# A fused transformer block on one core: a new list for the order of issue of all engines' work

## The chip, the core and the metric

The kernel runs on one core of a Trainium2 chip. Its engines work in parallel, each in the order in which its instructions were issued: TensorE (PE; its weight loads are shown apart as PEld), VectorE (DVE), ScalarE (ACT), GpSimd (POOL) and SyncE (SP), which here issues nearly all transfers. The metric is the device time of one execution in microseconds (us).

## What is computed

The block has 2048 rows of 512 numbers and a conditioning vector `c`. In short:

```
mod = silu(c) @ w_mod                      # six vectors: sa, ca, ga, sb, cb, gb
h   = layernorm(x) * (1 + ca) + sa
q, k, v = h @ wqkv                         # 32 heads of 16
logits[s, w] = q[s] . k[s - 2 w] / 4       # w = 0..7, masked where s - 2 w < 0
o   = softmax(logits) applied to v[s - 2 w]
x   = x + ga * (o @ wo)
h   = layernorm(x) * (1 + cb) + sb
x   = x + gb * ((gelu(h @ w_gate) * (h @ w_up)) @ w_down)      # 1792 hidden
```

Inputs, weights and output are bf16.

## The kernel before, in words

The rows are worked in four groups of 512, numbered 0 to 3 (`sg` in the code). Each group goes through the same chain of small steps. A step is an `Op`: one engine, a function that issues one or a few instructions, and a name (`fire`). The names below are those of the code, and a number behind the first dot is the group:

- `LN1.g.st0` to `st3` (L430, L431, DVE): statistics of a quarter of the rows. Some quarters are done on ACT instead: `sa`, `nm`, `sq` (L408, L414, L419). `vd` and `va` (L460, L465, DVE) add the epsilon, `rs` (L471, POOL) takes the power -1/2, `x0` to `x3` (L448, DVE) normalise.
- The transpose of the normalised rows: by PE for `LN1.1` and `LN2.0` (`t0`, `t1`, L484) and `LN1.0` (`th0` to `th3`, L514), by a transposing transfer from SP for the others (`.t`, L490). `.h0` to `.h3` apply scale and shift: on ACT (L532), on POOL for `LN1.2` (L530), on ACT and DVE for `LN1.0` (L549, L547).
- `qp.g.b.j` (L606, and L579 for the first ones): products for block b (0 = q, 1 = k, 2 = v), part j. `qkv.g.b.j` (L626, L628, L632, ACT) casts each out of PSUM.
- `vst` (L642) writes v to DRAM, `V4.g.0` to `.2` and `V4ld.g` (L651) read it back shifted.
- `pq.g.j` (L671, DVE): products of q and shifted k. `lp.g.j` and `lp.g` (L685, PE) sum them over the head with 32-wide products.
- Softmax: `mx` (L702), `z` (L708), `e` (L713, ACT), `s1` (L718), `ri` (L724), `p` (L729).
- `ptp.0` (L743, PE) spreads the weights for group 0; for groups 1 to 3 `est` (L757) and `ptl`, `pt` (L765) do it through DRAM.
- `pv.g.j` (L778, DVE): weights times v; `o.g.j` (L797, PE) sums them; `oT` (L808, ACT) casts them.
- `x1p` (L818, PE) and `x1` (L827, DVE): output projection and first residual. Then `LN2` as `LN1`.
- `g.g.f` and `u.g.f` (L851, PE), f = 0 to 13; `gl` and `ub` (L885, L892, ACT) take them out of PSUM; `hh` (L903, DVE) multiplies them.
- `y.g.c.0` and `.1` (L863, PE; `yl` L875 at the very end): the down projection in two halves of 7 products; `ot` (L910, `otl` L918, DVE): second residual; `sto` (L935, L926): the store.
- Apart from the groups: `w0` to `w16` (L217), PE warm-up products; `mp0` to `mp5` (L348, L305, L369, PE), the products with `w_mod`, with `mod01` (L355, DVE), `mod3`, `mod4`, `gc2`, `gc5` (ACT) behind them, and `gst`, `ga`, `gb` (SP), which spread the gates; `woS` (L391) and `WdS` (L386, DVE), which multiply the gates into `wo` and `w_down`; the loads `x0` to `x3`, `wm0` to `wm5`, `wqkv`, `wo`, `Wg`, `Wu`, `Wd` (SP).

Buffers are counted in slots that a step takes and gives back: among others four PSUM banks `mm` (for qp, mp, g, u, y), two `att` (o, x1p and transposes), five SBUF buffers for pq and pv, three each for `gl` and `ub`, sixteen for `hh`.

The chains are 135 generators (threads), numbered in the order in which they are spawned. The list `ORDER` (L19) holds 850 thread numbers. `run` takes the list from front to back and issues the next step of the thread named; the engines' queues are thereby written out by hand. A step's dependencies and slots are only asserted there:

```
for i in ORDER:
    op = nxt[i]
    assert all(name in self.done for name in op.after), (op.fire, op.after)
    for s in op.take:
        assert s.n > 0, op.fire
        s.n -= 1
    op.fn()
    for s in op.give:
        s.n += 1
    nxt[i] = next(self.threads[i], None)
```

What an engine waits for while it runs follows from the data and buffers of each instruction.

Of the kernel before, what the change touches and what calls it, by code (L numbers as in the profile page):

```python
# [16 lines left out]
PT_DMA = (1, 2, 3)  # L17

ORDER = [  # L19
# [965 lines left out]
```

## Time and profile before

| what | value |
|---|---|
| median of 3 runs | 238.06 us (238.01 to 238.08) |
| profiled execution: span from first to last instruction | 235.7 us |
| median less that span | 2.36 us |
| PE busy | 229.0 us (97%) |
| DVE busy | 170.0 us (72%) |
| ACT busy | 150.5 us (64%) |
| POOL busy | 23.6 us (10%) |

The page gives no time of the profiled execution beside its span. A group of instructions is named by the line that issued it, its engine, and the tiles that it writes and reads (`out<-in`); `[0.90 <-POOL rstd L471]` behind a row is the idle time of the engine before it, and what ended it. Matmuls overlap in the records, so a PE row's length is longer than the distance to the next one.

### The profile page before, as it was taken

What the parts mean: (1) busy time and instruction counts of PE and PEld (TensorE: products, weight loads), DVE (VectorE), ACT (ScalarE), POOL (GpSimd) and SP (SyncE); (2) the same over time, 40 slices, a digit from 0 to 9 for tenths busy, and PEclk for the clock granted to TensorE, in tenths of its full rate; (3) what the DMA queues carried; (4) which work ended last, traced back from release to release, by engine and by line L of the source; (5) the groups of instructions that cost most, each with busy time, mean ns of one, the idle gap of its engine ahead of it and who ended that gap; (6) DMA issues with size and microseconds to landing.
All of it is one profiled execution on the core that took longest, in us unless ns stands there. A gap on an engine that the chain in (4) does not pass through costs nothing.

```text
span 235.7 us, 3655 instructions
## 1 busy us (share of the span) xinstructions
PE 229.0 (97%) x1376; PEld 108.6 (46%) x1388; DVE 170.0 (72%) x240; ACT 150.5 (64%) x283; POOL 23.6 (10%) x43
## 2 busy tenths in 40 slices
PE   7899899999999999999999999999999999999995
PEld 2755355434644444443444444444444444444443
DVE  3898999999999999989899787259295421222222
ACT  4799978796997558943867592446737325667400
POOL 2525471000100000040000010000001000000000
PEclk9999999999999999999999999999999999999999
DMA  6997987999969929607301972520000061000011
GB/s 212 375 361 210 209 214 138 217 376 347 195 161 241 298 75 201 112 3 178 90 0 32 211 123 48 144 56 0 0 3 1 22 134 45 3 0 0 0 47 45
DMA packets 36265, 30.21 MB, mean 128 GB/s; under 512 B 14872, under 2 KB 34328, under 8 KB 36248
## 3 DMA queue, kind: packets, MB, share of 16 engines
q1 hardware_dynamic: 35968, 29.72, 49.7%
q8 instruction: 11, 0.18, 0.4%
q10 hardware_dynamic: 280, 0.26, 0.3%
q14 instruction: 6, 0.05, 0.1%
HBM read 22.37 MB, written 4.98 MB: 116 GB/s over the span
## 4 chain that ended last, share of the span: by engine, by line
PE 79%; DVE 10%; DMA 5%; POOL 3%; issue 1%; ACT 0%; DVEq 0%; POOLq 0%
PE g_ps L851 21%; PE u_ps L851 21%; PE y_ps L863 14%; PE qkv_ps L606 11%; PE x_ps L818 6%; DMA x<-in_A_x_dram 5%; DVE pq L671 4%; PE o_ps L797 3%; POOL rstd L471 3%; PE LTp L685 2%; DVE xn L448 1%; PE y_ps L875 1%; DVE pv L778 1%; DVE st L430 1%; DVE e L729 1%
## 5 line engine op out<-in xcount | busy, mean ns | idle before, releaser
L851 PE MATMUL g_ps<-h,Wg 128*128 128x512 bf16 x224 | 57.5, 379 | 0.0
L851 PE MATMUL u_ps<-h,Wu 128*128 128x512 bf16 x224 | 57.5, 379 | 0.0
L863 PE MATMUL y_ps<-Wd,hht 128*128 128x512 bf16 x203 | 45.6, 379 | 0.4
L885 ACT ACTIVATE gl<-g_ps 128x512 bf16<-128x512 f32 x56 | 33.7, 601 | 17.5 <-PE g_ps L851 15.4
L892 ACT CAST ub<-u_ps 128x512 bf16<-128x512 f32 x56 | 32.9, 587 | 16.2 <-PE u_ps L851 16.1
L606 PE MATMUL qkv_ps<-hT,wqkv 128*128 128x512 bf16 x180 | 41.0, 380 | 0.0
L903 DVE TENSOR_TENSOR hht<-gl,ub 128x512 bf16<-128x512 bf16 x56 | 23.0, 421 | 24.4 <-ACT ub L892 24.4
L778 DVE TENSOR_TENSOR pv<-PT,V 128x4096 bf16<-128x4096 bf16 x16 | 36.0, 2288 | 3.0 <-DMA PT<-escr 3.0
L671 DVE TENSOR_TENSOR pq<-qT,kT 128x4096 bf16<-128x4096 bf16 x16 | 36.4, 2296 | 0.0
L851 PEld LDWEIGHTS <-Wg 128*128 128x128 bf16 x224 | 21.7, 98 | 26.9 <-issue 1.3
L851 PEld LDWEIGHTS <-Wu 128*128 128x128 bf16 x224 | 21.7, 98 | 26.8 <-issue 0.8
L863 PEld LDWEIGHTS <-hht 128*128 128x128 bf16 x210 | 20.6, 98 | 24.7
L606 PEld LDWEIGHTS <-wqkv 128*128 128x128 bf16 x180 | 19.6, 114 | 18.6 <-issue 2.3
L471 POOL TENSOR_TENSOR rstd<-rstd,neghalf 128x4 f32<-128x4 f32 (+1 forms) x9 | 12.8, 1427 | 149.0 <-DVE rstd L460 77.6
L910 DVE TENSOR_TENSOR ot<-y_ps,x 128x512 bf16<-128x512 f32 x15 | 10.2, 690 | 20.0 <-PE y_ps L863 19.8
L532 ACT ACTIVATE h<-h,modT,scl 128x512 bf16<-128x512 bf16 x12 | 8.8, 805 | 20.3 <-DMA h<-xn 20.3
L818 PE MATMUL x_ps<-woP,oT 128*128 128x512 bf16 x60 | 15.1, 379 | 0.2
L430 DVE BATCH_NORM_STATS2 st<-x 128x6 f32<-128x512 bf16 x19 | 12.9, 677 | 3.1 <-DMA x<-in_A_x_dram 2.9
L827 DVE TENSOR_TENSOR x<-x_ps,x 128x512 bf16<-128x512 f32 x16 | 10.8, 688 | 5.4 <-PE x_ps L818 5.3
L808 ACT CAST oT<-o_ps 128x512 bf16<-128x512 f32 x16 | 8.8, 588 | 4.3 <-PE o_ps L797 4.3
L408 ACT ACTIVATE gl<-x 128x512 bf16<-128x512 bf16 x13 | 8.3, 645 | 3.2 <-DVE x L827 2.9
L685 PE MATMUL LTp<-pq,Mph 128*32 128x512 bf16 x128 | 9.1, 382 | 1.3 <-DVE pq L671 1.3
(85 smaller groups left out, 184.7 us busy)
## 6 DMA issues: line engine op xcount, KB each, us to landing
V<-vscr SPq DMA_DIRECT2D x12, 520.0 KB, 10.5
wm<-in_w_mod_dram SPq DMA_DIRECT2D x6, 512.0 KB, 5.3
vscr<-vT SPq DMA_DIRECT2D x4, 512.0 KB, 4.3
out_dram<-ot SPq DMA_DIRECT2D x15, 128.0 KB, 1.7
Wg<-in_B_w_gate_dram SPq DMA_DIRECT2D x1, 1792.0 KB, 9.8
Wu<-in_B_w_up_dram SPq DMA_DIRECT2D x1, 1792.0 KB
wqkv<-in_A_wqkv_dram SPq DMA_DIRECT2D x3, 512.0 KB, 8.8
x<-in_A_x_dram SPq DMA_DIRECT2D x3, 512.0 KB, 9.2
```

What stands on the lines that cost most here:

```text
L430: nc.vector.bn_stats(out=st[:], in_=src()[:, c4, :])
L471: nc.gpsimd.tensor_tensor(out=k["rstd"][:, a:b], in0=k["rstd"][:, a:b], in1=neghalf[:, a:b], op=ALU.pow)
L606: nc.tensor.matmul(ps[:], lhsT=wqkv[blk][:, dt, j::4], rhs=B["hT", sg][:, :, dt, :], start=(dt == 0), stop=(dt == DT - 1))
L671: nc.vector.tensor_tensor(out=pq[:], in0=_ap(B["qT", sg][:, j, :], [[0, W], [1, SG]]), in1=_ap(kT[:, j, sg % 3 * SG + 2:sg % 3 * SG + 2 + ...
L685: nc.tensor.matmul(B["LT", sg][H * g:H * g + H, 4 * t:4 * t + 4, :], lhsT=M[:], rhs=B["pq", sg, j][:, 4 * t:4 * t + 4, g * P:(g + 1) * P], ...
L778: nc.vector.tensor_tensor(out=t[:], in0=_ap(B["PT", sg][:, 0, :], [[SG, 2], [0, 4], [1, SG]]), in1=_ap(v[:, 0, j, :], [[8, 2], [4 * (SG + ...
L818: nc.tensor.matmul(ps[:], lhsT=B["oT", sg][:, j, c4::CPS] if sg else B["oT", sg][:, j, c4 * P:(c4 + 1) * P], rhs=woP[:, j, :], start=(j == ...
L851: nc.tensor.matmul(ps[:], lhsT=Wt[:, dt, ft * P:(ft + 1) * P], rhs=B["h2T", sg][:, :, dt, :], start=(dt == 0), stop=(dt == DT - 1))
L863: nc.tensor.matmul(ps[:], lhsT=B["hh", sg, ft][:, c4 * P:(c4 + 1) * P], rhs=B["Wd", ft // 4][:, ft % 4, :], start=(ft == 0), stop=(ft == F ...
L885: nc.scalar.activation(out=gl[:], in_=B["g", sg, ft][:], func=ACT.Gelu_apprx_tanh)
L892: nc.scalar.copy(out=ub[:], in_=B["u", sg, ft][:])
L903: nc.vector.tensor_tensor(out=hh[:], in0=B["gl", sg, ft][:], in1=B["ub", sg, ft][:], op=ALU.mult)
```

## The change

Only the list `ORDER` differs. It holds the same 850 entries in another order, found by a search that used each operation's duration as a trace shows it. No step, tile, transfer or wait in the code is added, removed or altered. The diff replaces 41 lines of numbers; its beginning:

```
@@ -17,41 +17,41 @@
 ORDER = [
-    23, 23, 23, 23, 23, 23, 23, 2, 33, 1, 23, 1, 0, 23, 0, 22, 31, 23, 23, 31, 31, 2, 33, 22, 23, 23, 22, 23,
-    33, 33, 33, 33, 2, 33, 23, 23, 22, 22, 22, 33, 34, 34, 34, 34, 35, 35, 22, 36, 3, 30, 23, 6, 35, 35, 4, 0,
...
+    23, 0, 0, 2, 33, 33, 23, 23, 23, 23, 23, 23, 23, 23, 23, 23, 1, 1, 22, 22, 23, 23, 23, 23, 31, 22, 31, 33,
+    33, 33, 34, 34, 33, 31, 33, 33, 34, 34, 0, 35, 23, 23, 35, 2, 2, 22, 22, 22, 22, 30, 35, 23, 35, 30, 30, 30,
...
```

Written out by step names, each engine's queue changes as follows (parts that stay as they were are left out; `..` stands for steps in between).

PE:

```
before: w13 w14 mp1 mp0 th0 th1 w15 th2 th3 w16 | qph.0 ..
after:  w13 th0 w14 w15 th1 mp1 mp0 th2 w16 th3 | qph.0 ..
before: qp.0.2.0 qp.0.2.1 qp.0.2.2 LN1.1.t0 qp.0.2.3 t1 mp2 mp3 qp.0.1.3 lp.0.0 qp.1.0.0 qp.1.1.0
        qp.1.2.0 qp.1.2.1 qp.1.2.2 lp.0.1 lp.0.2 lp.0 qp.1.2.3 qp.1.0.1 ..
after:  qp.0.2.0 LN1.1.t0 qp.0.2.1 qp.0.2.2 qp.0.2.3 t1 lp.0.0 mp2 qp.0.1.3 mp3 qp.1.0.0 qp.1.1.0
        lp.0.1 qp.1.2.0 qp.1.2.1 qp.1.2.2 qp.1.2.3 lp.0.2 lp.0 qp.1.0.1 ..
before: qp.1.1.3 qp.2.0.0 .. qp.2.2.2 ptp.0 qp.2.2.3 .. qp.2.1.2 lp.1.0 qp.2.0.3 qp.2.1.3 lp.1.1 o.0.0
        lp.1.2 o.0.1 qp.3.0.0 qp.3.1.0 o.0.2 o.0.3 .. qp.3.0.1 mp4 qp.3.1.1 ..
after:  qp.2.0.0 .. qp.2.2.1 qp.1.1.3 qp.2.2.2 ptp.0 lp.1.0 lp.1.1 qp.2.2.3 .. qp.2.0.3 mp5 o.0.0
        lp.1.2 o.0.1 mp4 qp.2.1.3 qp.3.0.0 qp.3.1.0 o.0.2 o.0.3 .. qp.3.0.1 qp.3.1.1 ..
before: u.0.8 o.1.1 o.1.2 lp.2.2 lp.2 o.1.3 g.0.9 x1p.1.0 x1p.1.1 u.0.9 x1p.1.2 x1p.1.3 g.0.10 ..
after:  u.0.8 g.0.9 o.1.1 o.1.2 lp.2.2 lp.2 o.1.3 u.0.9 x1p.1.0 x1p.1.1 g.0.10 x1p.1.2 x1p.1.3 ..
before: lp.3.0 lp.3.1 lp.3.2 g.1.0 .. u.1.6 g.1.7 o.2.0 o.2.1 lp.3 o.2.2 o.2.3 u.1.7 g.1.8 x1p.2.0 ..
after:  lp.3.0 lp.3.1 g.1.0 .. u.1.4 lp.3.2 o.2.0 o.2.1 g.1.5 .. u.1.6 o.2.2 lp.3 o.2.3 g.1.7 x1p.2.0 ..
before: y.1.2.1 y.1.3.0 y.1.3.1 g.2.0 .. u.2.5 o.3.0 .. o.3.3 g.2.6 .. x1p.3.0 .. x1p.3.3 g.2.8 ..
after:  y.1.2.1 g.2.0 o.3.0 .. o.3.3 u.2.0 g.2.1 x1p.3.0 .. x1p.3.3 .. u.2.3 y.1.3.0 y.1.3.1 g.2.4 ..
before: g.2.11 .. u.2.13 y.2.0.0 .. y.2.3.1 g.3.0 ..
after:  g.3.0 to g.3.3 and u.3.0 to u.3.3 spread between u.2.10 and y.2.2.0
```

DVE:

```
before: st2 LN1.0.vd2 va2 x0 x1 x2 x3 mod01 ..            after: st2 x0 x1 vd2 va2 x2 x3 mod01 ..
before: LN1.2.st1 st2 vd0 LN1.1.x0 x1 x2 LN1.2.va0 LN1.1.x3 pq.0.0 ..
after:  LN1.2.st1 LN1.1.x0 x1 x2 x3 LN1.2.st2 vd0 va0 pq.0.0 ..
(then the same, apart from one or two neighbours, up to pq.2.2)
before: pv.1.1 pv.1.2 pv.1.3 hh.0.5 mx.2 hh.0.6 hh.0.7 WdS0 x1.1.0 x1.1.1 WdS1 hh.0.8 ..
after:  pv.1.1 hh.0.5 pv.1.2 pv.1.3 WdS0 WdS1 WdS2 hh.0.6 hh.0.7 hh.0.8 x1.1.0 x1.1.1 mx.2 ..
before: z.2 LN2.1.va0 pq.3.1 LN2.1.x0 .. x3 ot.0.0 ot.0.1 s1.2 ri.2 p.2 pq.3.2 ot.0.2 ot.0.3 pq.3.3
        hh.1.0 hh.1.1 pv.2.0 hh.1.2 pv.2.1 pv.2.2 hh.1.3 hh.1.4 pv.2.3 hh.1.5 ..
after:  z.2 LN2.1.va0 LN2.1.x0 .. x3 s1.2 ri.2 p.2 ot.0.0 ot.0.1 pq.3.1 pq.3.2 ot.0.2 pq.3.3
        pv.2.0 hh.1.0 hh.1.1 hh.1.2 pv.2.1 hh.1.3 hh.1.4 pv.2.2 pv.2.3 hh.1.5 .. x1.2.0 ot.0.3 ..
after, from there: s1.3, ri.3, p.3 ahead of hh.1.7; pv.3.0 to pv.3.3 ahead of ot.1.0; ot.1.3 ahead of hh.2.2
```

ACT: `scT` ahead of `LN1.0.nm`; `LN1.2.sa3` ahead of the casts `qkv.0.0.j` (before: behind them); `LN1.1.h0`, `h1` ahead of `qkv.0.2.1`; `LN1.3.sq` ahead of `qkv.1.0.1`; `qkv.2.0.2`, `qkv.2.1.2` and `gc5` between `LN1.3.h1` and `h2`; `LN2.1.sa0`, `sa1` ahead of `gl.0.9`; `e.3` behind `gl.1.7` (before: behind `gl.1.9`); `oT.3.j` ahead of `gl.2.0`; `LN2.3.h0` to `h3` between `ub.2.6` and `gl.2.9`. There are seven changes of function between silu, exp and gelu in both lists.

SP:

```
before: .. x1 wqkv1 x2 wqkv2 wm2 wm3 x3 wo2 wo0 wo3 wo1 vst.0 LN1.2.t V4.0.0 gst2 V4.0.1 ga vst.1
        V4.0.2 V4ld.0 LN1.3.t vst.2 wm4 Wg Wu V4.1.0 V4.1.1 V4.1.2 est.1 V4ld.1 ptl.1 Wd0 wm5 Wd1 vst.3 ..
after:  .. x1 x2 wqkv1 wqkv2 wm2 wm3 wo3 x3 Wg vst.0 LN1.2.t V4.0.0 V4.0.1 vst.1 gst2 wo2
        V4.0.2 ga V4ld.0 wm5 LN1.3.t wm4 wo0 vst.2 wo1 Wu V4.1.0 V4.1.1 V4.1.2 vst.3 V4ld.1 gst5 est.1 Wd0 ptl.1 ..
```

Later on SP: `est.2` ahead of `sto.0.0`; `est.3` ahead of `V4ld.3`, and `ptl.3` ahead of `LN2.2.t`; the stores `sto.0.3` and `sto.1.3` go back. POOL's queue is the same in both.

66 rows, old and new, of the table ORDER are left out of this document.

## The prediction

> **What bounds the kernel now.** I read the page first, then the busy time by stretch, the chain of work that ended last, the waits, and the order of time around each wait of TensorE. From the page, and from the busy time by stretch (columns: stretch, length, then busy us and count of PE, PEld, DVE, ACT and POOL, granted clock, DMA share, GB/s):
>
> ```profile
> span 235.7 us, 3655 instructions
> PE 229.0 (97%) x1376; PEld 108.6 (46%) x1388; DVE 170.0 (72%) x240; ACT 150.5 (64%) x283; POOL 23.6 (10%) x43
> ```
>
> ```profile
> 20.00:98.00 78.00, 76.94 (x553) 36.46 (x552) 76.65 (x79) 63.72 (x133) 9.75 (x7) 1.00 0.89 218
> 112.00:233.00 121.00, 120.47 (x623) 55.42 (x629) 65.28 (x106) 64.59 (x105) 2.05 (x2) 1.00 0.21 48
> ```
>
> PE is busy nearly throughout, at a granted clock of 1.00. Until 98 us DVE is equally full (76.65 of 78 us), so there two engines pace the kernel together; after 112 us only PE does. A new order can't shorten PE's work. It can only take out PE's waits, and there are few. From the order of time and the chain:
>
> ```profile
> 27.03 1.05 PE L685 MATMUL LTp<-pq,Mph 128*32 128x512 bf16 x16
> 28.82 0.61 PE L685 MATMUL LTp<-pq,Mph 128*32 128x512 bf16 x8 [0.74 <-DVE pq L671]
> ```
>
> ```profile
> 50.92 0.61 PE L797 MATMUL o_ps<-pv,Msum 128*32 128x512 bf16 x8
> 51.75 0.62 PE L797 MATMUL o_ps<-pv,Msum 128*32 128x512 bf16 x8 [0.21 <-DVE pv L778]
> ```
>
> ```profile
> 110.50 1.05 PE L685 MATMUL LTp<-pq,Mph 128*32 128x512 bf16 x16
> 112.08 0.62 PE L685 MATMUL LTp<-pq,Mph 128*32 128x512 bf16 x8 [0.53 <-DVE pq L671]
> 112.63 1.04 PE L851 MATMUL g_ps<-h,Wg 128*128 128x512 bf16 x4
> ```
>
> ```profile
> 165.32 1.84 PE o_ps L797 x32
> 167.17 0.97 PE g_ps L851 x4
> 168.13 0.86 PE u_ps L851 x4
> ```
>
> A full step (four 128x512 products) takes 0.86 us from start to start. A narrow step (eight 32-wide products: lp, o) takes 0.43, and a group of narrow steps costs about 0.2 more in entering (1.84 for four is 0.11 over 4 x 0.43) and leaving (0.97 against 0.86). So lp.0 lost 28.82 - 27.03 - 0.86 = 0.92 us waiting for pq.0.3, o.0.3 lost 51.75 - 50.92 - 0.43 = 0.40 for pv.0.3, and lp.3.2 lost 112.08 - 110.50 - 0.86 = 0.72 for pq.3.2. Together 2.0 us: about all that an order can win behind the head.
>
> **The change, stage by stage.** I keep count by PE's lateness: the start of a step less the PE work queued ahead of it.
>
> *Head (0 to 13 us).* DVE now makes LN1.0.x0 and x1 ahead of the two small steps vd2 and va2; the transposes th0, th1 stand ahead of mp1, mp0; and the load of x2 is issued ahead of wqkv1.
>
> ```profile
> 7.01 0.73 DVE L448 TENSOR_SCALAR xn<-x,mv,rstd 128x512 bf16<-128x512 bf16 x2
> 7.17 0.80 POOL L471 TENSOR_TENSOR rstd<-rstd,neghalf 128x2 f32<-128x2 f32 x1 [0.34 <-DVE rstd L465]
> 8.01 0.41 DVE L448 TENSOR_SCALAR xn<-x,mv,rstd 128x512 bf16<-128x512 bf16 x1 [0.27 <-POOL rstd L471]
> 8.66 0.17 DVE L355 TENSOR_TENSOR mod<-modT_ps,c 128x8 f32<-128x8 f32 x1
> 9.02 1.77 DVE L547 TENSOR_SCALAR hT<-hTp,mod 128x256 bf16<-128x256 bf16 x5 [0.19 <-PE hTp L514]
> 9.81 2.78 PE L579 MATMUL qkv_ps<-hT,wqkv 128*128 128x256 bf16 x24
> 10.84 0.69 DVE L430 BATCH_NORM_STATS2 st<-x 128x6 f32<-128x512 bf16 x1
> 12.55 2.03 ACT L626 CAST qT<-qkv_ps 128x512 bf16<-128x512 f32 x4
> 14.65 0.66 ACT L408 ACTIVATE gl<-x 128x512 bf16<-128x512 bf16 x1
> ```
>
> POOL's power (0.80) can start only after x0 and x1, so 0.65 later; x0 itself moves up by 0.1. x2 then starts at about 8.67 instead of 8.01, mod01 at 9.34, the five hT writes at 9.55, and LN1.1.st0 at 11.19 instead of 10.84: DVE is 0.35 late. PE's first product starts at 10.0 instead of 9.81. On ACT LN1.2.sa3 (0.66) moves ahead of the four casts, so the casts start at 13.44 instead of 12.55, the first bank comes free at 14.0, and PE, which has four, waits 0.57 for it. The later landing of wqkv1 lies under that wait. Cost: DVE 0.35; PE 0.19 + 0.57.
>
> *13 to 98 us.* lp.0.0 and lp.0.1 come earlier, and qp.1.2.3 moves ahead of lp.0.2 and lp.0, whose wait (0.92) is then filled: by qp.1.0.1 PE is 0.26 ahead. But DVE's work here is the same, in almost the same order, and full, so what is tied to it comes no sooner:
>
> ```profile
> 38.17 1.23 DVE L729 TENSOR_TENSOR e<-LTp,rinv 128x1024 bf16<-128x1024 f32 x1
> 39.85 0.62 PE L743 MATMUL PTp<-e,ident 128*32 128x256 bf16 x16
> 62.22 0.73 DVE L448 TENSOR_SCALAR xn<-x,mv,rstd 128x512 bf16<-128x512 bf16 x2
> 63.00 1.06 PE L484 MATMUL hTp<-ident,xn 128*128 128x128 bf16 x16
> ```
>
> p.0 ends at 39.40 + 0.35 = 39.75, so ptp.0 starts at 39.8, as before (39.85). Mod products mp4, mp5 and the late qp.2.1.3 fill the wait at o.0.3 (0.40), but LN2.0.x3 ends at 62.95 + 0.35 = 63.3, so the transposes LN2.0 end 0.3 later in time with 0.22 more done (mp5). Through 98 us (hh early or late, g.0.9 ahead of o.1.1, WdS ahead) PE keeps a backlog of steps whose inputs exist. DVE's 0.35 goes into the 1.35 us that it idles in this stretch. I take the net at y.0.0.0 as -0.1 (ends: -0.4, if the transposes don't wait; +0.5, if ACT's moved casts each cost one 0.5 us bank wait).
>
> *DMA, the same stage.* Wg (1792 KB) moves from behind LN1.3.t to ahead of vst.0; three wo loads move behind it, wm5 ahead of LN1.3.t. All are on SP's queue, and whatever stands behind them is pushed back.
>
> ```profile
> 10.00:20.00 10.00, 10.00 (x68) 6.68 (x67) 9.52 (x24) 9.64 (x25) 3.94 (x4) 1.00 1.07 344
> 20.00:22.00 2.00, 2.00 (x44) 1.22 (x40) 1.22 (x4) 2.00 (x4) 0.74 (x1) 1.00 0.19 60
> 40.00:42.00 2.00, 2.00 (x24) 1.07 (x17) 2.00 (x4) 2.00 (x4) 0.00 (x0) 1.00 0.02 4
> 49.00:54.00 5.00, 4.74 (x35) 1.93 (x33) 5.00 (x4) 4.26 (x10) 0.00 (x0) 1.00 1.02 412
> ```
>
> ```profile
> 40.75 1.68 SPq L490 DMA_TRANSPOSE hT<-xn  x1
> 45.14 2.94 ACT L532 ACTIVATE hT<-hT,mod 128x512 bf16<-128x512 bf16 x4 [1.22 <-DMA hT<-xn]
> ```
>
> The queue runs empty at 20 and at 40 us. At 412 GB/s Wg takes 4.45 us; less 1.1 for the wo loads (384 KB at the 344 GB/s of 10 to 20 us) it ends 3.4 after 20.0, and 2 of that were empty: vst.0 and all V loads come 1.4 later. That, wm5 (1.4) and wo2 (0.35) must fit into the 2 empty us before LN1.3.t: 1.1 over. The queue's mean share from 20 to 98 us is 0.89, so the 18 us between hold some 2 us in which it could do more; I take 0.9 of them. So LN1.3.t lands 0.2 later, plus DVE's 0.35 on its input, and ACT's h0 starts at 45.65. Ends: 0 and +4.2 (if Wg moves at the mean rate, 218 GB/s). PE's qp.3.0.0 waits for it and starts at 49.75 (before: 49.08, with 0.6 less done); a later landing is paid one to one. The Trainium skill, page "DMA: Bandwidth & Descriptors", section "Where 436 GB/s comes from", says that loads from HBM are bound at about 358 GB/s for a core. By it Wg would take 5.1 us, 0.65 more, and the time would be some 0.4 worse than my sum; the 412 above stands against it.
>
> *98 to 128 us, where the gain is.* LN2.1.x0 to x3 and softmax 2 now stand ahead of pq.3.1; lp.3.2 goes behind u.1.4 with o.2.0 and o.2.1; ot.0.3 goes far back.
>
> ```profile
> 37.30 1.01 POOL L471 TENSOR_TENSOR rstd<-rstd,neghalf 128x4 f32<-128x4 f32 x1 [3.43 <-DVE rstd L465]
> 100.92 2.92 POOL L471 TENSOR_TENSOR rstd<-rstd,neghalf 128x4 f32<-128x4 f32 x1 [39.39 <-DVE rstd L465]
> 103.88 1.38 DVE L448 TENSOR_SCALAR xn<-x,sums,rstd 128x512 bf16<-128x512 bf16 x4 [0.90 <-POOL rstd L471]
> 109.74 2.94 ACT L532 ACTIVATE h<-h,modT,scl 128x512 bf16<-128x512 bf16 x4 [6.89 <-DMA h<-xn]
> 109.75 2.28 DVE L671 TENSOR_TENSOR pq<-qT,kT 128x4096 bf16<-128x4096 bf16 x1
> 116.92 0.42 DVE L903 TENSOR_TENSOR hht<-gl,ub 128x512 bf16<-128x512 bf16 x1 [1.15 <-ACT ub L892]
> 124.87 2.29 DVE L778 TENSOR_TENSOR pv<-PT,V 128x4096 bf16<-128x4096 bf16 x1
> ```
>
> Without pq beside it the power takes 1.01, not 2.92: x0 starts at 102.1 instead of 103.88, and h is ready 1.9 sooner, at 110.8. DVE's idle stays about 1 us. From x0 DVE needs 109.75 - 103.88 = 5.87 us for the same steps before its next pq, so pq.3.1 runs from 107.97 to 110.25, in time for lp.3.1 (110.8), and g.1.0 starts at 111.35. Before, it started at 112.63 with 0.43 more done: 0.85 won. Lost again: one more narrow group, 0.2. pv.2.3 ends at 125.85 (before 127.16; less the 1.15 of idle and ot.0.3's 0.6, plus some 0.4 of waits for the power and for ub.1.4) and o.2.3 is reached at 125.9. Net -0.65; ends -0.85 (no extra group cost) and 0 (o.2.3 waits 0.65 for DVE). ot.0.3's bank is held till 130 us, and three banks are enough while a cast (0.6) is shorter than a step (0.86).
>
> *128 us to the end.* e.3, p.3, pv.3.x and o.3.x come some 15 us earlier, x1p.3.x likewise; y.1.3 and ot.1.3 move, and g.3.0 to g.3.3 go between y.2.x. Cost nothing: PE has 120.47 of 121 us before and the same steps after, DVE only 65.28. Its cover is PE's backlog; were pv.3.3 later than about 153.5, each us would cost one. Number of table loads (7), and the tail from y.3.0.0 on, are unchanged.
>
> Sum: -0.1 (to 98 us), -0.65, and some 0.15 added for arrivals that I found in time by under 0.1: -0.6. The page gives only the span of the profiled execution; the median, 238.06, is 2.36 above it, and I keep that: 235.1 + 2.36 = 237.5.
>
> **Rivals.**
> *Nothing to measure.* o.2.3 meets pv.2.3 with 0.05 to spare, and DVE's lateness of 0.35 must vanish before 98 us. If it doesn't, o.2.3 waits that much, and 0.2 elsewhere: 238.0. For it: both paces are the same engines as before. Against: the idle that takes it up is in the trace.
> *Slower, by the DMA queue.* The transpose LN1.3.t lands over 2 us late behind Wg and wm5; ACT stands before h0 with casts behind it and PE's four banks full, so PE loses 1.7 at qp.3.0.0, of which 0.3 is taken up by 63 us: -0.6 + 1.4 = +0.8, 238.9. It decides from a lateness of about 1.1. For it: LN1.3.t was ACT's wait already (1.22). Against: the empty 2 us.
> *Slower, by POOL.* LN1.2.h3 on POOL and pq.1.1 on DVE overlap. If POOL stands still under pq, as the power did (2.92 against 1.01), qp.2.0.0 waits 2 us: 239.0. The Trainium skill, page "GPSIMD Engine Reference", section "1. Specifications", has POOL share its SBUF interfaces with such DVE instructions. In this trace all POOL work before it is tied to the same pq, and the overlap stays.
> *More.* DVE isn't late and no transition is added: -1.2, 236.9.
>
> **How the numbers follow.** Forecast 0.40; nothing to measure 0.27; DMA 0.20; POOL 0.06; more 0.07. A measurement tells 0.2%, 0.48 us, from no change. The forecast lies just past it and counts a fifth to "same", a little of "nothing" counts to faster: faster 0.42, same 0.32, slower 0.26. The range reaches from the best case to the DMA rival, 236.9 to 239.0.
>
> **What would show it.** Right: lp.0 without its wait; LN1.1.st0 at about 11.2; the power before LN2.1.x0 near 1 us; g.1.0 at about 111.3; no wait at lp.3.2; PE full from 112 us on. Wrong: ACT before LN1.3.h0 much past 46 us, a PE gap before qp.2.0.0 or qp.3.0.0, o.2.3 or any o.3.x waiting for DVE, DVE waiting for V or PT.

## The result, and the profile after

The changed kernel is slower. It takes 240.94 us in the median (239.72 to 241.11), against 238.03 for the kernel before: a ratio of 1.0115, with a 95% interval of 1.0092 to 1.0138. The forecast was 237.5 with a range of 236.9 to 239.0: the time went the other way and lies above the range. A second measurement (below, `after_again`) gave 1.0093 (1.0060 to 1.0126). In the tables below the medians are of all executions and the ratios leave out disturbed ones, so the two can differ a little.

From the page of the changed kernel:

```profile
span 238.8 us, 3651 instructions
...
PE 231.0 (97%) x1377; PEld 109.0 (46%) x1388; DVE 170.2 (71%) x240; ACT 148.7 (62%) x283; POOL 18.6 (8%) x43
```

The profiled execution took 241.05 us, 2.25 over its span, as before (2.36); so the whole difference is in the span, 238.8 against 235.7. I follow it by PE's lateness, the start of a step less the PE work queued ahead of it, as the prediction did. The table is of one execution of each kernel:

| step | before | after | after less before |
|---|---|---|---|
| first product `qph.0` | 4.17 | 4.07 | -0.1 |
| `qp.1.0.1` (after's start 29.82) | 5.79 | 5.34 | -0.45 |
| `o.0.0` (46.72) | 6.34 | 6.03 | -0.3 |
| `qp.3.2.0` (56.70) | 7.08 | 10.85 | +3.8 |
| `g.0.0` (70.40) | 7.46 | 11.14 | +3.7 |
| `y.0.0.0` (102.02) | 8.00 | 11.70 | +3.7 |
| `y.1.0.0` (145.85) | 9.23 | 12.36 | +3.1 |
| last product | 9.47 | 12.60 | +3.1 |

So the new order is ahead until 46 us, loses 4.1 us in the ten that follow, and wins 0.6 back between 98 and 146. The stage of the loss, in busy time by stretch (columns: stretch, length, then busy us and count of PE, PEld, DVE, ACT and POOL, granted clock, DMA share, GB/s), first before, then after:

```profile
44.00:57.00 13.00, 12.73 (x103) 5.01 (x102) 13.00 (x9) 9.46 (x19) 0.00 (x0) 1.00 1.00 361
```

```profile
20.00:22.00 2.00, 2.00 (x37) 1.24 (x35) 1.33 (x5) 1.98 (x4) 0.63 (x1) 1.00 1.03 406
...
44.00:57.00 13.00, 10.19 (x97) 4.23 (x96) 12.30 (x6) 6.96 (x14) 0.00 (x0) 0.87 1.07 305
...
48.00:50.00 2.00, 0.61 (x8) 0.12 (x7) 2.00 (x2) 2.00 (x6) 0.00 (x0) 1.00 1.05 342
50.00:52.00 2.00, 0.97 (x18) 0.70 (x19) 2.00 (x2) 2.00 (x4) 0.00 (x0) 0.81 1.03 322
52.00:54.00 2.00, 2.00 (x7) 0.61 (x5) 1.67 (x2) 0.84 (x2) 0.00 (x0) 0.50 0.98 347
54.00:56.00 2.00, 2.00 (x15) 0.79 (x17) 2.00 (x2) 0.59 (x1) 0.00 (x0) 0.83 1.02 403
```

The queue, empty at 20 to 22 us before, is now full there with Wg (406 GB/s). At 44 to 57 us PE is busy for 10.19 us of 13 instead of 12.73. From 48 to 51 it hardly works, and from about 51 to 55 it works at half its clock: the granted clock falls to 0.50. The order of time in the changed kernel shows what it waits for (start, length; in brackets the idle time ahead and what ended it):

```profile
22.67 4.38 SPq L490 DMA_TRANSPOSE hT<-xn  x1
...
40.71 4.54 SPq L490 DMA_TRANSPOSE hT<-xn  x1
...
44.37 8.90 DVE L778 TENSOR_TENSOR pv<-PT,V 128x4096 bf16<-128x4096 bf16 x4 [1.53 <-DMA V<-vscr]
...
47.34 1.52 ACT L532 ACTIVATE hT<-hT,mod 128x512 bf16<-128x512 bf16 x2 [3.09 <-DMA hT<-xn]
...
48.92 0.61 PE L797 MATMUL o_ps<-pv,Msum 128*32 128x512 bf16 x8 [1.16 <-DVE pv L778]
...
51.03 0.57 PE L305 MATMUL modT_ps<-scT,wm 128*128 128x1 bf16 x16 [1.49 <-DMA wm<-in_w_mod_dram]
...
51.46 4.33 PE L606 MATMUL qkv_ps<-hT,wqkv 128*128 128x512 bf16 x12
```

In the kernel before, the first of the two transposes and `pv.0.0` stand so:

```profile
22.23 1.68 SPq L490 DMA_TRANSPOSE hT<-xn  x1
...
42.80 4.50 DVE L778 TENSOR_TENSOR pv<-PT,V 128x4096 bf16<-128x4096 bf16 x2
```

Three transfers are late at once. V is late for `pv.0.0` (44.37 against 42.80), and behind it PE waits 1.16 us at `o.0.1`. The transpose LN1.3.t is late for ACT's `h0` (47.34 against 45.14). The weights wm4 are late for `mp4`, which the change put ahead of `qp.2.1.3`, so that PE stands 1.49 us more. Then come three steps of four products, x12, that take 4.33 us instead of 2.76 (the same group in `a_fill` below). And SP stands for 4.4 and 4.5 us at the issue of the two transposes, where it stood for 1.68.

This standing makes LN1.3.t late, for its issue starts when it did before (40.71 against 40.75). Where the transfer that was issued ahead of it on SP's queue is still in flight, the issue ends close to that transfer's landing (times in us; in the kernel before it had landed already, and the issue took 1.68):

| run | LN1.3.t: issue starts, ends | issued ahead of it, lands | `h0` starts |
|---|---|---|---|
| before | 40.75, 42.43 | V4ld.0, 40.99 | 45.14 |
| after | 40.71, 45.25 | wm5, 45.46 | 47.34 |
| `a_wg_late` (below) | 40.83, 43.79 | wm5, 43.96 | 45.77 |
| `a_wm5_late` (below) | 40.88, 43.92 | V4ld.0, 44.09 | 45.75 |

In `a_ga_behind` and `a_wg_est` end and landing are 0.6 and 0.4 apart. LN1.2.t behind vst.0 shows the same: after, its issue ends at 27.05 and vst.0 lands at 27.39; before, 23.91 and 24.14. It isn't the whole rule: a later transpose in the changed kernel holds SP from 107.07 to 110.27, though the transfer ahead of it had landed at 103.43.

The other stage in which the two differ is 98 to 146 us. Before, and then after:

```profile
98.32 12.25 PE L863 MATMUL y_ps<-Wd,hht 128*128 128x512 bf16 x54
...
142.72 3.62 PE L863 MATMUL y_ps<-Wd,hht 128*128 128x512 bf16 x15
```

```profile
102.02 12.25 PE L863 MATMUL y_ps<-Wd,hht 128*128 128x512 bf16 x54
...
104.62 1.01 POOL L471 TENSOR_TENSOR rstd<-rstd,neghalf 128x4 f32<-128x4 f32 x1 [38.86 <-DVE rstd L465]
...
123.92 0.62 PE L685 MATMUL LTp<-pq,Mph 128*32 128x512 bf16 x8
...
145.85 0.38 PE L863 MATMUL y_ps<-Wd,hht 128*128 128x512 bf16 x1
```

From `y.0.0.0` to `y.1.0.0`, the same steps, it takes 145.85 - 102.02 = 43.83 us instead of 44.40: 0.57 won. The power takes 1.01 us, not 2.92, and `lp.3.2` (123.92) no longer waits.

### The profile page after: what moved, and what is told of

It is laid out like the page before. It is cut to its first block, busy times and chain, and to the rows that moved or that the text cites. A ratio compares the mean times of both kernels' runs of the same rounds, so it can differ in the third digit from the quotient of the medians.

```text
span 238.8 us, 3651 instructions
## 1 busy us (share of the span) xinstructions
PE 231.0 (97%) x1377; PEld 109.0 (46%) x1388; DVE 170.2 (71%) x240; ACT 148.7 (62%) x283; POOL 18.6 (8%) x43
## 4 chain that ended last, share of the span: by engine, by line
PE 89%; DMA 6%; ACT 2%; SPq 1%; issue 1%; DVE 0%
PE g_ps L851 20%; PE u_ps L851 20%; PE y_ps L863 19%; PE qkv_ps L606 16%; PE x_ps L818 6%; DMA x<-in_A_x_dram 3%; PE LTp L685 3%; PE o_ps L797 3%; DMA wm<-in_w_mod_dram 2%; PE y_ps L875 1%; PE hTp L484 1%; ACT gl L408 1%; ACT oT L808 0%; SPq L245 0%; PE modT_ps L305 0%
## 5 line engine op out<-in xcount | busy, mean ns | idle before, releaser
L863 PE MATMUL y_ps<-Wd,hht 128*128 128x512 bf16 x204 | 46.1, 379 | 0.3
L903 DVE TENSOR_TENSOR hht<-gl,ub 128x512 bf16<-128x512 bf16 x56 | 22.3, 420 | 29.8 <-ACT ub L892 29.6
L606 PE MATMUL qkv_ps<-hT,wqkv 128*128 128x512 bf16 x180 | 42.5, 390 | 0.4 <-ACT qT L626 0.4
L471 POOL TENSOR_TENSOR rstd<-rstd,neghalf 128x4 f32<-128x4 f32 (+1 forms) x9 | 10.5, 1168 | 139.7 <-DVE rstd L465 75.7
L626 ACT CAST qT<-qkv_ps 128x512 bf16<-128x512 f32 x16 | 9.2, 596 | 3.1 <-PE qkv_ps L606 3.1
```

Source lines behind the costliest of these rows:

```text
L606: nc.tensor.matmul(ps[:], lhsT=wqkv[blk][:, dt, j::4], rhs=B["hT", sg][:, :, dt, :], start=(dt == 0), stop=(dt == DT - 1))
L863: nc.tensor.matmul(ps[:], lhsT=B["hh", sg, ft][:, c4 * P:(c4 + 1) * P], rhs=B["Wd", ft // 4][:, ft % 4, :], start=(ft == 0), stop=(ft == F ...
L903: nc.vector.tensor_tensor(out=hh[:], in0=B["gl", sg, ft][:], in1=B["ub", sg, ft][:], op=ALU.mult)
```

## The experiments

My theory after the result: the load Wg (1792 KB), put ahead of vst.0, takes 4.4 us of the DMA engines in a stage that had none to spare, so that V, LN1.3.t and wm4 all come late, and PE's gap then halves its clock. The rivals: it is `ga`, at which SP stands for 5.2 us ahead of V4ld.0; it is `wm5`, put ahead of LN1.3.t; it is `mp4`, put ahead of `qp.2.1.3`; or the new order of PE, DVE and ACT costs the time itself. All kernels below compute the whole block. In some of them the list is a line longer or code is added, so that their line numbers are up to 4 higher.

| label | what it is | median us | ratio to before | 95% interval |
|---|---|---|---|---|
| `a_wg_late` | after, Wg late | 240.68 | 1.0113 | 1.0083 to 1.0143 |
| `b_wg_early` | before, Wg early | 242.30 | 1.0183 | 1.0170 to 1.0196 |
| `a_ga_behind` | after, ga behind V4ld.0 | 240.04 | 1.0060 | 1.0035 to 1.0085 |
| `a_mp4_late` | after, mp4 late | 239.58 | 1.0076 | 1.0060 to 1.0093 |
| `a_wm5_late` | after, wm5 and mp5 late | 238.90 | 1.0034 | 1.0021 to 1.0046 |
| `a_fill` | after, six products in PE's gap | 239.93 | 1.0080 | 1.0066 to 1.0094 |
| `a_sp_back` | after, SP's queue as before | 237.81 | 0.9989 | 0.9979 to 0.9999 |
| `b_98` | before to 98 us, then after | 237.60 | 0.9984 | 0.9974 to 0.9994 |
| `b_wg_half` | before, half of Wg early | 239.93 | 1.0077 | 1.0051 to 1.0102 |
| `a_wg_est` | after, Wg late, est.1 ahead | 238.02 | 0.9994 | 0.9978 to 1.0010 |
| `a_sp_back2` | as a_sp_back, two steps more | 237.46 | 0.9978 | 0.9963 to 0.9993 |
| `b_98_lp` | as b_98, qp.1.2.3 moved | 237.49 | 0.9974 | 0.9960 to 0.9987 |
| `b_wg_act` | before, Wg early on ACT's queue | 242.32 | 1.0180 | 1.0152 to 1.0208 |
| `b_wg_behind_t` | before, Wg behind LN1.2.t | 243.18 | 1.0210 | 1.0181 to 1.0239 |
| `a_wg_act` | after, Wg on ACT's queue | 241.37 | 1.0144 | 1.0103 to 1.0185 |
| `after_again` | after, measured again | 241.15 | 1.0093 | 1.0060 to 1.0126 |

**Wg alone, put early.**

```
 SP (before):  .. wo1
+              Wg
               vst.0 LN1.2.t V4.0.0 .. LN1.3.t vst.2 wm4
-              Wg
               Wu ..
```

> The kernel before with one step moved: Wg is issued ahead of vst.0, all else as it was. Queue theory: vst.0 lands at 27 to 28 instead of 24.1, V4ld.0 and LN1.3.t 1.5 to 3 us later than 41.0 and 45.05, and the time is 239 to 241. Rivals (ga, or wm5 and mp4, which are where they were before): 237.8 to 238.3, since the empty stretches at 20 and 40 us take Wg up.

It costs 4.4 us (1.0183), more than the whole change. The transposing transfer's issue now takes 7.21 us, and everything behind it on SP is late:

```profile
21.95 7.21 SPq L491 DMA_TRANSPOSE hT<-xn  x1
...
47.15 8.90 DVE L779 TENSOR_TENSOR pv<-PT,V 128x4096 bf16<-128x4096 bf16 x4 [2.95 <-issue]
48.63 2.93 ACT L533 ACTIVATE hT<-hT,mod 128x512 bf16<-128x512 bf16 x4 [2.78 <-DMA hT<-xn]
```

`pv.0.0` starts 4.35 later than before and `h0` 3.5. So this one step is enough for a loss of this size, with `ga`, `wm5` and `mp4` where they stood before.

**Wg alone, put back.**

```
 SP (after):  .. x3
-             Wg
              vst.0 .. LN1.3.t wm4 wo0 vst.2 wo1
+             Wg
              Wu V4.1.0 V4.1.1 V4.1.2 vst.3 V4ld.1 gst5 est.1 Wd0 ptl.1.0 ..
```

> The changed kernel with one step moved: Wg (1792 KB) is issued behind wo1, just ahead of Wu, where the kernel before had it, and no longer ahead of vst.0. Queue theory (Wg in front pushes vst.0, the V loads, LN1.3.t and wm4 back, and PE pays at 46 to 57 us): vst.0 lands at about 24, V4ld.0 at 41 to 42 instead of 44.3, LN1.3.t at 45 to 45.5 instead of 47.25; PE's lateness at g.0.0 falls from 11.14 to about 7.1 and the time to 236.9 to 237.6, below both kernels. Rival by ga (SP stands 5.2 us before ga with V4ld.0 behind it): V4ld.0 still lands past 43.5, 239.5 to 240.9. Rival by mp4 (PE waits for wm4 ahead of qp.2.1.3): wm4 is still late behind wm5 and wo2, 239.5 to 240.5.

The loss at 46 to 57 us is gone: `h0` starts at 45.77, `pv.0.0` at 42.88, and PE's lateness at `LN2.0.t0` is 7.41 (before 7.46, after 11.10).

```profile
42.88 8.90 DVE L778 TENSOR_TENSOR pv<-PT,V 128x4096 bf16<-128x4096 bf16 x4
...
45.77 1.52 ACT L532 ACTIVATE hT<-hT,mod 128x512 bf16<-128x512 bf16 x2 [1.41 <-DMA hT<-xn]
```

But the time is hardly better than the changed kernel's. It lies in the range of the rival by `ga`, whose sign did not come (V4ld.0 landed at 42.76, not past 43.5): 2.7 us are lost at another place that I hadn't foreseen.

```profile
67.20 0.35 SPq L757 DMA_DIRECT2D escr<-e  x1
...
74.89 2.57 SPq L765 DMA_DIRECT2D PT<-escr  x4
...
79.58 2.29 DVE L778 TENSOR_TENSOR pv<-PT,V 128x4096 bf16<-128x4096 bf16 x1 [2.60 <-DMA gB<-gscr]
```

(The row names gB as the last to arrive, but `pv.1.0` doesn't read gB; it needs PT.) The write `est.1` is issued at 67.20, and its reads only at 74.89, when it has landed. Ahead of it in the new SP order stand Wg, Wu, vst.3, V4ld.1 and gst5. In the changed kernel est.1's reads followed it after 2.3 us (70.59 and 72.91). So the two ends of the new transfer order belong together: the early Wg had made room for vst.3 and others ahead of est.1.

**Wg back, and what stood ahead of est.1 put behind its reads.**

```
 SP (a_wg_late):  .. V4.1.2
-                 vst.3 V4ld.1 gst5
                  est.1
+                 V4ld.1
-                 Wd0
                  ptl.1.0 ptl.1.1 ptl.1.2 pt.1.1
+                 Wd0 vst.3 gst5
                  gb ..
```

> The changed kernel with Wg issued behind wo1 (as in the kernel with Wg alone put back, 240.7), and behind that the transfers that stand ahead of est.1 or of its reads moved behind them: V4ld.1 behind est.1, and Wd0, vst.3 and gst5 behind pt.1.1. Queue theory: est.1 lands 2 to 3 us after its issue instead of 7.3, ptl.1.0 is issued by 71, pv.1.0 waits under 0.3: 237.6 to 238.4, and the runs scatter less. Rival (pv.1.0's wait came of something else, gB or the earlier lateness): 239.5 to 240.9.

The ratio is 0.9994 and `pv.1.0` no longer waits; ptl.1.0 is issued at 71.42. The reading of the second loss holds, although est.1 still takes longer than I expected (3.8 us from issue to the reads).

```profile
67.66 0.36 SPq L757 DMA_DIRECT2D escr<-e  x1
...
71.42 2.53 SPq L765 DMA_DIRECT2D PT<-escr  x4
...
77.36 2.28 DVE L778 TENSOR_TENSOR pv<-PT,V 128x4096 bf16<-128x4096 bf16 x1
```

**ga, wm5 and mp4, one at a time.**

```
 a_ga_behind, SP:  .. V4.0.2
-                  ga
                   V4ld.0
+                  ga
                   wm5 LN1.3.t ..
 a_mp4_late, PE:   .. o.0.1
-                  mp4
                   qp.2.1.3 .. qp.3.0.1
+                  mp4
                   qp.3.1.1 ..           (ACT: mod4 behind qkv.3.0.1)
 a_wm5_late, SP:   .. V4ld.0
-                  wm5
                   LN1.3.t wm4 wo0 vst.2 wo1
+                  wm5
                   Wu ..                 (PE: mp5 behind qp.3.0.3, ACT: gc5 behind qkv.3.0.3)
```

> The changed kernel with one step moved: ga, which makes SP wait for gst2's landing (32.31 to 37.53), is issued behind V4ld.0 instead of ahead of it. Queue theory: V4ld.0 is issued 5 us sooner, but the bytes ahead of it and of LN1.3.t are the same, LN1.3.t lands at 46.5 or later: 240.0 to 240.9. Rival by ga: V4ld.0 lands by 41, pv.0.0 starts at about 42.8 again, and with it PE's loss at o.0.0 and o.0.1 goes: 238 to 239.

> The changed kernel with mp4 (the product that waits 1.49 us for wm4) put back behind qp.3.0.1, and mod4 with it. Queue theory: PE does qp.2.1.3 at 49.5, then waits for LN1.3.h0 all the same (h0 at 47.3, its four steps and the casts behind it); 0.3 to 1.0 won, 240.0 to 240.6. Rival by mp4: with mp4 gone PE has no gap over 1.5 us, the clock stays at 1.00, and qp.3.0.0 starts at about 50.5: 238 to 239.

> The changed kernel with wm5 (512 KB) issued behind wo1 instead of ahead of LN1.3.t, and mp5 with its cast behind qp.3.0.3; Wg stays in front. Queue theory, in which bytes count: LN1.3.t and wm4 land 1.0 to 1.4 sooner (h0 at about 46), V4ld.0 as late as it was (44.3): 239.0 to 240.5. Rival (wm5 is the main thing): h0 at 45.2 and no loss past 1 us at 46 to 57 us, 237.5 to 238.5.

Only `wm5` wins clearly. With `ga` behind (1.0060) `pv.0.0` starts at 43.48 instead of 44.37 and `h0` stays at 47.32; but its executions scatter from 238.07 to 243.46, and its interval, like that of `a_mp4_late`, overlaps with the second measurement of the changed kernel. With `wm5` behind (1.0034) it is the other way round:

```profile
44.17 8.90 DVE L778 TENSOR_TENSOR pv<-PT,V 128x4096 bf16<-128x4096 bf16 x4 [1.15 <-ACT qT L626]
45.75 1.52 ACT L532 ACTIVATE hT<-hT,mod 128x512 bf16<-128x512 bf16 x2 [1.36 <-DMA hT<-xn]
```

`h0` is 1.6 earlier and the kernel wins about 2 us of the 2.7, a little more than the 0.4 to 1.9 that I expected of 512 KB. With `mp4` late (1.0076) the next wait shows: PE reaches `x1p.0.0` and stands there for the gate multiply, which waits for a wo load that was also moved behind:

```profile
55.16 1.22 DVE L391 TENSOR_TENSOR woP<-woP,gB 128x2048 bf16<-128x2048 bf16 x1 [1.80 <-DMA woP<-in_A_wo_dram]
56.45 1.90 PE L818 MATMUL x_ps<-woP,oT 128*128 128x512 bf16 x8 [1.43 <-DVE woP L391]
```

So none of the three is the whole cause, and each theory was half right. I read them as three places at which one backlog is paid; their parts don't add up to the loss, and no run separates them fully.

**The clock.** Six products that nobody reads go into PE's queue ahead of `mp4`'s, to fill the gap:

```
@@ in cols(b)
-            ps = T("mm", [P, 4], F32, "modT_ps")
+            ps = T("mm", [P, D], F32, "modT_ps")
             B["mp", b] = ps
+            for _ in range(6 * (b == 4)):
+                nc.tensor.matmul(ps[:], lhsT=wqkv[0][:, 0, 0:P], rhs=wqkv[0][:, 0, :], start=True, stop=True)
```

> The changed kernel with six products of 128x512 that nobody reads put into PE's queue ahead of mp4's products (they need no wm4), so that PE works through most of the 1.49 us in which it stands for wm4. Clock theory (the half clock at 51 to 55 us is the price of PE's gaps and is 1.3 to 1.6 of the loss): granted clock 1.00 at 52 to 54 us, qp.2.1.3 to qp.3.1.0 in 0.86 each, 239.3 to 239.7. Rival (the clock costs nothing that the next wait, for h and woS, would not have cost): 240.6 to 241.1.

```profile
50.00:52.00 2.00, 1.84 (x21) 0.80 (x19) 2.00 (x2) 2.00 (x5) 0.00 (x0) 1.00 1.07 319
52.00:54.00 2.00, 2.00 (x20) 1.15 (x17) 1.93 (x1) 1.50 (x4) 0.00 (x0) 1.00 1.02 302
```

```profile
50.13 1.47 PE L304 MATMUL modT_ps<-wqkv 128*128 128x512 bf16 x5
...
52.12 2.76 PE L608 MATMUL qkv_ps<-hT,wqkv 128*128 128x512 bf16 x12
```

The clock stays at 1.00 and the three steps take 2.76 us. The median is 1.0 us below the changed kernel's first one, less than expected, and the interval overlaps with that of its second measurement. The changed kernel's own executions are the better evidence. Measured twice, six of them show a mean clock of 1.000 and take 239.28 us in the mean (238.43 to 240.38); seven show 0.993 and take 241.21 (240.82 to 241.75); three show 0.986 and take 243.03 to 243.55. A mean of 0.993 is 3.3 us at half clock (2 x 0.007 x 238), about the stretch in the profile (51 to 55 us), and it costs PE some 1.7; 0.986 is twice that. So the clock after the gap makes most of the scatter and, where it comes, 1.9 us of the loss; at full clock the changed kernel is still some 1.3 us slower than the kernel before. The mean alone doesn't say where the half clock lies: in the profiled execution of `b_98`, also at 0.993, it is at 9 to 12 us. And the filled kernel, at full clock, is 0.6 slower than the changed kernel's executions at full clock; why is open. The Trainium skill, page "TensorE: Matmul & The Clock Gate", Part 1, says that TensorE falls to half its clock after an idle window of about 3.4 us, and that the window runs freely, so that it varies from run to run. The length and the scatter agree: by the rows of the changed kernel above the half clock lasts (0.19 + 0.50 + 0.17) x 2 / 0.5 = 3.4 us. An idle window isn't what the trace shows, for PE was busy for 0.61 us between 48 and 50.

> The changed kernel as it is, on the chip of the other three. All theories: 239.7 to 241.1 as measured, with the half clock at 52 to 54 us in most runs.

This run is the second of the two measurements. Its executions scatter more than I expected, from 238.43 up, for the reason just given.

**Is it the bytes, or SP standing at the transpose?** Half of Wg first:

```
 loads (b_wg_early):
-    ld(Wg[:], wg_v), fire="Wg"
+    ld(Wg[:, 0:2, :], wg_v[:, 0:2, :]), fire="Wg"
     and, ahead of Wu's transfer in the step Wu:
+    nc.sync.dma_start(out=Wg[:, 2:4, :], in_=wg_v[:, 2:4, :])
```

> The kernel before with only half of Wg (896 KB, two of its four row blocks) issued ahead of vst.0; the other half goes just ahead of Wu, behind wm4. Queue theory with the slack that the profile of before shows (queue empty for about 2 us at 20 to 22 us; 896 KB take 2.2 us at 412 GB/s): vst.0 lands at 24 to 25, LN1.3.t and V4ld.0 within 0.5 of 45.1 and 41.0, 237.8 to 238.6, so that the loss of 4.4 with all of Wg in front is a threshold and not in proportion. Rival (any load in front of vst.0 costs by its bytes from the first one on): half of 4.4, 239.5 to 240.5.

I was wrong here, and the rival right: half the bytes cost 1.8 us, not under 0.6. At this place there is no threshold of that size. The empty queue at 20 to 22 us is used, but an empty stretch comes back later:

```profile
20.00:22.00 2.00, 2.00 (x45) 1.44 (x44) 1.10 (x3) 1.96 (x5) 1.52 (x1) 1.00 1.04 277
...
26.00:28.00 2.00, 2.00 (x13) 0.90 (x15) 2.00 (x2) 0.88 (x2) 0.00 (x0) 1.00 0.27 35
```

```profile
23.00 5.06 SPq L494 DMA_TRANSPOSE hT<-xn  x1
...
45.76 8.90 DVE L782 TENSOR_TENSOR pv<-PT,V 128x4096 bf16<-128x4096 bf16 x4 [1.82 <-issue]
```

SP stands at LN1.2.t until 28.06 with the V reads behind it, and at 26 to 28 the engines move only 35 GB/s. That suggested a new theory: SP's standing is the price, not the bytes. Three runs test it, two with Wg on ACT's queue, one with Wg on SP's but behind the transpose.

```
 b_wg_act:       Wg issued by nc.scalar.dma_start behind the cast qkv.0.2.1, not on SP's queue
 a_wg_act:       the same in the changed kernel
 b_wg_behind_t:  SP (before):  .. vst.0 LN1.2.t
+                              Wg
                               V4.0.0 .. wm4
-                              Wg
                               Wu ..
```

> The kernel before with Wg started at about 19 us from ACT's queue (behind the cast qkv.0.2.1) instead of at 44.5 us from SP's. Same bytes at the same time as in the kernel with Wg in front (242.3), but no longer ahead of the transpose LN1.2.t on SP's queue. SP theory (the transpose's issue stands until what is ahead of it on its queue is through, and the V reads stand behind it): LN1.2.t's issue takes 1.7 to 2.5 us instead of 7.2, V4.0.0 is issued by 25.5 instead of 29.5, 238.5 to 240.0. Bytes theory (the 16 DMA engines are shared, Wg takes 4.4 us of them wherever it is issued): 241.5 to 242.8.

> The changed kernel with Wg started at about 20 us from ACT's queue (behind the cast qkv.0.2.1), no longer ahead of vst.0 and LN1.2.t on SP's. SP theory: LN1.2.t's issue takes under 2.5 us instead of 4.4, V4.0.0 is issued by 25.5 instead of 27.5, 238.0 to 239.5. Bytes theory: as the changed kernel, 240.0 to 241.1.

> The kernel before with Wg on SP's queue right behind the transpose LN1.2.t, ahead of V4.0.0. SP theory: the transpose is issued in 1.7 us and lands at 26.6 as before, qp.2.0.0 doesn't wait (lateness 5.8 there, 7.5 with Wg in front); the V reads lose Wg's bytes less the slack that they have, pv.0.0 at 44 to 46: 239.5 to 241.0. Bytes theory: V4ld.0 as late as with Wg in front, pv.0.0 at 47, 241.5 to 242.5.

The new theory falls. From ACT's queue Wg costs the same (1.0180 against 1.0183), and the transpose on SP's queue stands as long:

```profile
21.96 7.06 SPq L490 DMA_TRANSPOSE hT<-xn  x1
```

In the changed kernel it wins nothing either (1.0144). Behind the transpose Wg costs no less (1.0210): LN1.2.t is issued at once, but now the V reads and the next transpose pay. SP waits at `ga` until 37.47 for gst2 to land (before: until 30.43), and the last V reads, which stand behind it, are issued at 38.54 instead of 31.71.

```profile
22.52 1.99 SPq L490 DMA_TRANSPOSE hT<-xn  x1
...
37.47 0.36 SPq L323 DMA_DIRECT2D gB<-gscr  x1
...
41.03 6.90 SPq L490 DMA_TRANSPOSE hT<-xn  x1
...
48.43 8.90 DVE L778 TENSOR_TENSOR pv<-PT,V 128x4096 bf16<-128x4096 bf16 x4 [5.26 <-ACT kT L628]
49.91 2.94 ACT L532 ACTIVATE hT<-hT,mod 128x512 bf16<-128x512 bf16 x4 [2.46 <-DMA hT<-xn]
```

So in the order of the kernel before Wg's bytes are paid for wherever they are issued between 13 and 25 us: 896 KB cost 1.8 us and 1792 KB 4.3 to 5.0, which is about what they take at 412 GB/s (2.2 and 4.45). The Trainium skill says so too of the queue: page "DMA: Bandwidth & Descriptors", section "Issuing engines are not separate DMA queues", has transfers of all issuing engines run on the same 16 DMA engines and interleave. This case agrees (242.32 and 242.30). But the bytes alone don't set the price. In `a_wm5_late` all of Wg is as early, among the other transfers of the changed kernel, and that kernel is only 0.8 us slower than before. Which of the other transfers makes the difference, no run separates.

That LN1.2.t stands for so long because it is behind Wg on SP's queue is refuted. What fits is the landing of vst.0, the transfer issued just ahead of it: with Wg on ACT's queue in the changed kernel the issue ends at 27.59 and vst.0 lands at 27.88; with Wg behind the transpose, 24.52 and 24.60. So Wg would hold the transpose up by making vst.0 late, from either queue; no run tests this by itself.

**The new order without its transfer order.**

```
 SP (after): up to Wd3 in the order of the kernel before, but x2 ahead of wqkv1, ga behind V4ld.0,
             gst2 behind V4.0.1, wm5 ahead of Wd0
 PE, ACT (after): mp4 behind qp.3.0.1, mod4 behind qkv.3.0.1
 a_sp_back:   mp5 behind g.0.5, gc5 behind gl.0.5
 a_sp_back2:  mp5 behind lp.2.1, gc5 behind gl.0.6; LN1.2.sa3 behind scB, LN1.2.nm and sq3 behind qkv.0.1.0
```

> The changed kernel with SP's queue put back, up to Wd3, to the order of the kernel before (the four wo loads ahead of vst.0; vst.2, wm4, Wg, Wu behind LN1.3.t; est.1 and its four reads ahead of the wm5, Wd and vst.3 transfers), x2 still ahead of wqkv1 and ga behind V4ld.0; mp4 and mp5 with their casts go back behind qp.3.0.1 and g.0.5, since their weights come later. PE, DVE, ACT and POOL keep the new order otherwise. Queue theory: the loss at 46 to 57 us is gone and none comes at 75 to 82 us (where the kernel with Wg alone put back lost 2.7 at pv.1.0, behind est.1's late landing); the gains of the new order are left, 0.4 to 45 us and 0.57 at 98 to 128 us: 236.7 to 237.4, below both kernels. Rival (the new order of PE and ACT itself costs time, by banks or by h0 late): 238.0 or more, with PE waiting at 46 to 57 us although V4ld.0 lands by 41.

> The changed kernel with SP's queue put back as in the run at 237.8, and two more steps put back: mp5 and its cast behind lp.2.1 and gl.0.6, where the kernel before had them, and on ACT the three LN1.2 steps of the head behind scB and qkv.0.1.0, so that the casts of the first step group start first. Ledger of PE: the 0.35 at mp5 and the 0.53 for a bank at qp.0.1.0 are won, 236.9 to 237.3. Rival (until 98 us DVE sets the pace and PE's waits are made good at lp.1): only the 0.35 or nothing, 237.4 to 237.8.

With SP's queue back the kernel is faster than both, though than the one before by only 0.1%: 0.9989, and with two more steps back 0.9978 (237.46 us). The rival that the order of PE and ACT costs the time is refuted, and `a_wg_est`, which keeps that order without any step put back (0.9994), says so too. In `a_sp_back2` the stage of the loss is clean:

```profile
40.87 1.67 SPq L490 DMA_TRANSPOSE hT<-xn  x1
...
42.93 8.89 DVE L778 TENSOR_TENSOR pv<-PT,V 128x4096 bf16<-128x4096 bf16 x4
...
45.26 1.52 ACT L532 ACTIVATE hT<-hT,mod 128x512 bf16<-128x512 bf16 x2 [0.87 <-DMA hT<-xn]
```

But the times are 0.4 over the first expectation and in the rival's range for the second: PE's lateness at `y.0.0.0` is 8.05, as before (8.00). The gain comes from behind 98 us.

**The stage behind 98 us alone, and the wait at lp.0 alone.**

```
 b_98:     each engine's order as before up to 98.3 us, from there as after
 b_98_lp:  b_98, and on PE
               qp.1.2.2
+              qp.1.2.3
               lp.0.1 lp.0.2 lp.0
-              qp.1.2.3
               qp.1.0.1
```

> The kernel before with each engine's order kept up to 98.3 us and the new order from there on (LN2.1.x0 to x3 and softmax 2 ahead of pq.3.1, lp.3.2 behind u.1.4, ot.0.3 late, e.3 and o.3.x early). The prediction's step for 98 to 128 us: 0.5 to 0.65 won, none lost behind 128: 237.3 to 237.5, g.1.0 at about 111.5 and no wait at lp.3.2. Rival (the 0.57 that the changed kernel won there came of its 3.7 us of lateness, which gave LN2.1.t and PT's round trip slack): 237.8 to 238.2.

> The kernel before up to 98.3 us and the new order behind it (the run at 237.6), with one step of PE moved: qp.1.2.3 ahead of lp.0.1, so that it fills the wait of 0.92 for pq.0.3 ahead of lp.0. Prediction's ledger of PE: up to 0.9 won, 236.7 to 237.0. Rival (DVE sets the pace of this stage and PE's lead is gone by lp.1, which waits for pq.1.3): nothing won, 237.3 to 237.8, with PE's lateness at g.0.0 as in the kernel before, about 7.5.

`b_98` is faster than before by 0.16% (0.06 to 0.26). From `y.0.0.0` to `y.1.0.0` it takes the same 43.83 us as the changed kernel:

```profile
99.06 12.25 PE L863 MATMUL y_ps<-Wd,hht 128*128 128x512 bf16 x54
...
142.89 3.40 PE L863 MATMUL y_ps<-Wd,hht 128*128 128x512 bf16 x14
```

So this part of the change is worth 0.57 us of PE's time by itself, 0.4 in the measured time, and doesn't come of lateness. `b_98_lp` fills the wait of 0.92 at `lp.0`, and PE is 0.7 ahead at `qp.1.0.1` (lateness 5.08 against 5.79). The lead is gone six steps on:

```profile
28.09 1.53 PE L685 MATMUL LTp<-pq,Mph 128*32 128x512 bf16 x24
...
35.48 4.51 PE L606 MATMUL qkv_ps<-hT,wqkv 128*128 128x512 bf16 x20 [0.55 <-ACT qT L626]
```

`lp.0.1` to `lp.0` run without a gap, but at `qp.2.0.0` PE waits 0.55 for a bank, and at `g.0.0` its lateness is 7.62 (before 7.46). The time, 0.9974, can't be told from that of `b_98`. Here a wait of PE that is filled is paid at the next meeting with ACT or DVE.

## Why the prediction was wrong

By its own steps:

- *Head.* Right in kind, with no weight. The wait for a bank came (lateness +0.6 at `qp.0.1.0`, 0.57 forecast). DVE's 0.35 came relative to `LN1.0.x0` (`LN1.1.st0` starts 4.15 behind it instead of 3.83), but x0 started 0.31 earlier in the profiled execution and hid it; LN1.1.st0 was at 10.85, not at 11.19.
- *13 to 98 us without the transfers, -0.1.* Right: `a_sp_back2`, in which nearly only PE, DVE and ACT have the new order, reaches `y.0.0.0` with a lateness of 8.05 against 8.00. `lp.0`'s wait went as forecast, and as `b_98_lp` shows, brought nothing.
- *DMA, the step that failed.* The prediction let Wg, wm5 and wo2 disappear in 2 us of empty queue and in 0.9 of the us "in which it could do more". It had vst.0 and the V loads 1.4 late; vst.0 landed 3.25 later (27.39 against 24.14), and the first V read was issued at 27.46 instead of 24.15. It had LN1.3.t 0.2 late and `h0` at 45.65; `h0` started at 47.34, 2.2 later than before. Two things were wrong. The slack was not there to be used so: half of Wg, 2.2 us of transfer, already cost 1.8. The empty stretches at 20 and 40 us end with vst.0 and LN1.3.t, which are issued as soon as their inputs exist (ACT's last v cast ends at 20.57 and vst.0 is issued at 20.60; LN1.3.x3 ends at 40.69 and LN1.3.t is issued at 40.75). So a load moved ahead of them can run through the gap into them; this is argued from the order of events, not tested. And SP's longer stand at the two transposes, 4.4 and 4.5 us instead of 1.68, with the V reads and wm4 behind it, was no term of the prediction. The prediction also priced LN1.3.t alone. V4ld.0's consumer `pv.0.0` (1.57 later), wm4's `mp4` (a wait of 1.49) and the wo loads (1.8 in `a_mp4_late`) were not in it, though all stand on the same queue.
- *"A later landing is paid one to one."* In most executions it was paid more than so: PE's gap brought the half clock, 1.57 us in the profile (4.33 against 2.76), about 1.9 us between executions at 1.000 and at 0.993. No step of the prediction had the clock in it.
- *The Trainium skill's 358 GB/s.* The worse time that followed from it was still too good by 3. Here the queue moved 406 GB/s at 20 to 22 us, with Wg in it; the rate was not the error.
- *98 to 128 us, -0.65.* Right in mechanism and nearly in size: 0.57, with the power at 1.01 us and no wait at `lp.3.2`. `b_98` shows it by itself.
- *128 us to the end, 0.* Right: lateness grows by 0.24 before and after.

Of the rivals, "slower, by the DMA queue" had the place and the sign right (0.20 chance, 238.9) and two sizes wrong: it took 1.7 us at `qp.3.0.0` for a lateness of over 2, where 4.1 were lost in the stage, and it let the loss begin only at a lateness of about 1.1. Its 238.9 is near the 239.28 of the executions at full clock; the clock that took the others further was in no rival. "Slower, by POOL" didn't happen: LN1.2.h3 ended at 33.76, before at 33.87.
